# The first 1 MB of an expert's weights as two transfers of 64 partitions, one on each hardware queue

## The chip, the cores and the metric

The kernel runs on one core of a Trainium2 chip. The metric is the time of one execution on the device in microseconds (us); medians of several runs are quoted. A ratio is the mean time of one kernel's runs over the mean of the other's of the same rounds, so it is not quite the ratio of the medians that stand beside it.

## The reference

Windowed attention (8 batches, 8 heads, 576 positions, head size 64; four heads with a plain window, four with a dilated one) is followed by a soft mixture of experts with 8 experts of 4 slots each:

```python
attn_out = _attn_ref(q, k, v)                      # f32, [8, 8, 576, 64]
x = attn_out.transpose(0, 2, 1, 3).reshape(4608, 512)
logits = x @ phi                                   # phi [512, 32]
d = softmax(logits, axis=0); slot_input = (d.T @ x).reshape(8, 4, 512)
for e in range(8):                                 # w1 [8, 512, 1024], w2 [8, 1024, 512]
    slot_out[e] = np.maximum(slot_input[e] @ w1[e], 0.0) @ w2[e]
return softmax(logits, axis=1) @ slot_out.reshape(32, 512)
```

All inputs are f32 in HBM. The weights are 33.5 MB of them, q, k and v together 28.3 MB.

## The kernel before

GpSimd's software queue loads nearly everything and casts f32 to bf16 in flight. A small scheduler in Python orders the instructions of each engine; the order is fixed when the program is built. The first half of the columns of w1 of expert 0 is an exception: it is loaded as f32 on SyncE's hardware queue, which can start before GpSimd has issued anything (0.74 against 1.23 us), into a place that w2 of expert 0 fills much later. ScalarE casts it from there:

```python
def w1_rows(e):
    return moe_w1[e].rearrange("(p four) f -> p (four f)", four=4)   # 128 rows of 4096 f32
...
op(SP, lambda: spq.dma_start(
    af(w2off(0), [[1, 2048]]),            # f32 view, 128 partitions x 8 KB
    w1_rows(0)[:, :2048]), .1, -200.0,
   kind="dma", nbytes=1 << 20, sem=sem("s_w1f"), writes=b_w2[0], name="w1f")
for x in range(2):
    op(ACT, lambda x=x: act.activation(
        a(o_w1 + 1024 * x, [[1, 1024]]), af(w2off(0) + 2048 * x, [[1, 1024]]), ACTF.Copy),
        1.1, -200.0, reads=b_w2[0], writes=[b_w1[0]], name=f"w1c{x}")
...
wq += [w1_piece(e, 2 if e == 0 else 0) for e in range(8)]   # the rest of w1, on GpSimd
```

The softmax here doesn't subtract the row's maximum and nothing guards it: scores larger than these inputs give would overflow.

Of the kernel before, what the change touches and what calls it, by code (L numbers as in the profile page):

```python
# [58 lines left out]
class Sched:  # L59
# [8 lines left out]
    def op(self, eng, fn, dur, prio, reads=(), writes=(), rmw=(), after=(), banks=(), name="",  # L68
           kind="c", nbytes=0, rate=422e3, lag=0.0, sem=None, tail=False):
        o = Op()  # L70
        o.eng, o.fn, o.dur, o.prio, o.name = eng, fn, dur, prio, name
        o.kind, o.bytes, o.rate, o.lag, o.sem, o.tail = kind, nbytes, rate, lag, sem, tail
        o.deps, o.succ = set(), []
        o.banks, o.opens, o.ord = [], [], None
        o.seq = len(self.ops)
        for a in after:
            if a is not None:
                o.deps.add(a)
        for b in reads:
            o.deps.update(b.w)  # L80
            b.r.append(o)
        for b in writes:
            if b.r:
                b.prev = b.w + b.r
                b.w, b.r = [], []
            o.deps.update(b.prev)
            b.w.append(o)
        for b in rmw:
            o.deps.update(b.prev)
            o.deps.update(b.w)  # L90
            o.deps.update(b.r)
            b.w.append(o)
        for b in list(reads) + list(writes) + list(rmw) + list(banks):
            if isinstance(b, Bank) and b not in o.banks:
                o.banks.append(b)
                if b.left == 0:
                    o.opens.append(b)
                b.left += 1
        o.deps.discard(o)
        self.ops.append(o)  # L100
        return o
# [99 lines left out]
def bass_dilated_sliding_attn__then__soft_moe_slots_kernel(  # L201
# [66 lines left out]
    def af(off, dims, p0=0, pn=128):  # L268
        return AP(ar_f.tensor, (p0 * NBF + off) // 2, [[NBF // 2, pn]] + dims)
# [12 lines left out]
    op = sc.op  # L282
    PE, ACT, DVE, POOL, SP = "PE", "ACT", "DVE", "POOL", "SP"
    pe, act, dve, pool, spq = nc.tensor, nc.scalar, nc.vector, nc.gpsimd, nc.sync
# [26 lines left out]
    b_w2 = [[Buf(f"w2{e}{s}") for s in range(2)] for e in range(8)]  # L311
# [6 lines left out]
    def w2off(e):  # L318
        return o_w2 + e * 8 * DM if e < 5 else o_stg + (e - 5) * 8 * DM


    def sem(n):
        return [nc.alloc_semaphore(n), 0]
# [39 lines left out]
    def w1_rows(e):  # L363
        return moe_w1[e].rearrange("(p four) f -> p (four f)", four=4)
# [28 lines left out]
    def load_w(n):  # L393
# [11 lines left out]
                   writes=list(wr) + rd + ([x for y in b_kqv[0] for x in y] if name[:2] == "w2" and e in (3, 4) else []))  # L405


    op(SP, lambda: spq.dma_start(
        af(w2off(0), [[1, 2048]]),
        w1_rows(0)[:, :2048]), .1, -200.0,  # L410
       kind="dma", nbytes=1 << 20, sem=sem("s_w1f"), writes=b_w2[0], name="w1f")
    for x in range(2):
        op(ACT, lambda x=x: act.activation(
            a(o_w1 + 1024 * x, [[1, 1024]]), af(w2off(0) + 2048 * x, [[1, 1024]]), ACTF.Copy),
# [398 lines left out]
    for x, y in zip(dma_order, dma_order[1:]):  # L813
# [7 lines left out]
       writes=[b_rcol], name="cs")  # L821
# [17 lines left out]
    for x in range(2):  # L839
# [12 lines left out]
        for g in range(2):  # L852
# [5 lines left out]
            writes=[b_hsb[x], b_p[0], b_p[1]], name=f"RL{x}")  # L858
# [20 lines left out]
    def l2(es, x, col, n, cs=range(8), bufs=None):  # L879
# [22 lines left out]
       name="SOx")  # L902
# [153 lines left out]
```

## Time and profile before

| | before |
|---|---|
| median time | 177.12 us (176.88 to 177.25, 4 runs) |
| span of the profiled run | 175.2 us |
| DMA | 41.26 MB written by 14,388 packets, near 213 GB/s from 5 to 145 us |

The prediction below works with 177.03 us, the median of the first three of these runs. It shows the lines of the profile that carry the argument. One view more is needed later. It is the queue view of the first 12 us, whose columns are packets, MB, and the time that their packets took as a share of 16 engines over those 12 us:

```profile
q0 software_dynamic: 710, 1.47, 64.8%
q1 hardware_dynamic: 144, 1.05, 26.4%
```

The hardware queue's row is the transfer in question: 1.05 MB took 26.4% of 12 us, so 3.17 us of all 16 engines.

### The profile page before, as it was taken

To read this page: it belongs to the slowest core of one execution; us is meant where nothing else is said; L and a number is where in the kernel's file an instruction comes from. 1 tells how busy PE (TensorE), PEld (TensorE's weight loads), DVE (VectorE), ACT (ScalarE), POOL (GpSimd) and SP (SyncE) were. 2 spreads that over 40 slices of the span, in tenths; PEclk is the share of its full clock that TensorE was granted. 3 is DMA by queue.
4 is the path that set the end of the run, shared out by engine and by line. 5 is a ranking of instruction groups with operands and counts; after the bars stand their busy time and mean duration, and the time that the engine had idled before them with its cause. 6 is when DMAs were issued, how large, how long until landed. Compare 5 with 4: busy or idle time off the path is not lost.

```text
span 175.2 us, 4785 instructions
## 1 busy us (share of the span) xinstructions
PE 127.4 (73%) x2102; PEld 86.0 (49%) x2102; DVE 120.7 (69%) x220; ACT 105.1 (60%) x165; POOL 44.5 (25%) x90
## 2 busy tenths in 40 slices
PE   0008667969998998998988997999776766898000
PEld 0005535746766866776756766776343323442000
DVE  6899497978998998998698798349430002699300
ACT  2404763797978969969868968965603001599000
POOL 7659502406234053027200014940000000000000
PEclk9999995699999999999999999999999999999655
DMA  6999999999999999999999999999999999999997
GB/s 191 228 210 217 211 214 208 219 210 213 216 211 214 217 213 207 218 211 217 213 209 216 217 213 221 215 219 211 209 223 215 210 192 189 270 343 418 449 423 299
DMA packets 14388, 41.26 MB, mean 236 GB/s; under 512 B 1696, under 2 KB 7328, under 8 KB 12064
## 3 DMA queue, kind: packets, MB, share of 16 engines
q0 software_dynamic: 10512, 30.41, 88.3%
q1 hardware_dynamic: 3856, 10.55, 15.7%
q8 instruction: 16, 0.26, 0.5%
q14 instruction: 4, 0.03, 0.0%
HBM read 61.93 MB, written 9.44 MB: 407 GB/s over the span
## 4 chain that ended last, share of the span: by engine, by line
DMA 33%; DVE 24%; PE 22%; ACT 7%; POOL 5%; issue 3%; POOLq 0%; DVEq 0%
DMA ar<-in_moe_w_dram 21%; DMA ar<-in_v_dram 12%; PE ps L529 6%; DVE ar L497 6%; DVE ar L945 6%; ACT ar L568 4%; POOL ar L381 3%; DVE ar L503 3%; PE ps L590 2%; PE ps L713 2%; PE ps L536 2%; DVE ar L634 2%; PE ps L623 2%; PE ps L546 2%; DVE ar L454 2%
## 5 line engine op out<-in xcount | busy, mean ns | idle before, releaser
L568 ACT ACTIVATE ar<-ps 128x1152 bf16<-128x1152 f32 (+1 forms) x32 | 37.9, 1186 | 21.5 <-PE ps L553 10.9
L529 PE MATMUL ps<-ar 128*128 128x320 bf16 (+1 forms) x128 | 23.2, 306 | 16.1 <-DVE ar L503 13.8
L497 DVE STREAM_TRANSPOSE ar<-ar 128x576 uint32<-128x576 uint32 x28 | 32.8, 1237 | 0.6 <-DMA ar<-in_v_dram 0.6
L634 DVE TENSOR_TENSOR ar<-ps,fs 96x768 bf16<-96x768 f32 (+1 forms) x32 | 26.3, 822 | 1.1
L596 ACT ACTIVATE ar<-ps 128x768 bf16<-128x768 bf16 x32 | 24.8, 809 | 3.6 <-PE ps L590 3.1
L529 PEld LDWEIGHTS ps<-ar 128*128 128x128 bf16 x128 | 10.8, 100 | 20.9 <-POOL ar L427 13.7
L623 PE MATMUL ps<-ar 128*128 128x65 bf16 x320 | 15.2, 195 | 3.4 <-ACT ar L568 2.1
L590 PE MATMUL ps<-ar 128*128 128x128 bf16 x192 | 15.8, 229 | 2.4 <-DVE ar L634 2.1
L503 DVE STREAM_TRANSPOSE ar<-ar 128x576 uint32<-128x576 uint32 x12 | 14.6, 1241 | 1.8 <-DMA ar<-in_q_dram 1.8
L623 PEld LDWEIGHTS ps<-ar 128*128 128x128 bf16 x320 | 12.1, 98 | 6.7 <-ACT ar L568 2.9
L345 POOL DMA_DIRECT2D ar<-in_k_dram x14 | 7.5, 541 | 30.5 <-DVE ar L497 15.6
L942 ACT ACTIVATE ar<-ps,fs 128x512 f32<-128x512 f32 (+1 forms) x23 | 11.4, 636 | 5.7 <-PE ps L934 5.7
L590 PEld LDWEIGHTS ps<-ar 128*128 128x128 bf16 x192 | 12.7, 118 | 3.7 <-DVE ar L634 2.3
L630 DVE RECIPROCAL fs<-ps 96x12 f32<-96x12 f32 (+1 forms) x32 | 6.5, 203 | 10.9 <-PE ps L623 10.6
L885 PE MATMUL ps<-ar 128*32 128x512 bf16 (+1 forms) x76 | 10.8, 347 | 4.3 <-DMA ar<-in_moe_w_dram 3.3
L945 DVE TENSOR_SCALAR ar<-ps,fs 128x512 f32<-128x512 f32 (+1 forms) x23 | 12.7, 627 | 1.0 <-PE ps L934 1.0
L934 PE MATMUL ps<-ar 128*128 128x512 bf16 (+1 forms) x46 | 10.2, 346 | 1.1 <-DVE ar L909 1.0
L343 POOL DMA_DIRECT2D ar<-in_q_dram x16 | 8.8, 549 | 6.1 <-DVE ar L509 6.1
L713 PE MATMUL ps<-ar 128*128 128x288 bf16 x64 | 9.8, 299 | 0.7 <-ACT ar L697 0.7
L693 ACT ACTIVATE ar<-ps 128x1024 bf16<-128x1024 bf16 x8 | 8.2, 1030 | 3.3 <-PE ps L680 3.3
L690 ACT ACTIVATE ar<-ps 128x576 bf16<-128x576 bf16 x16 | 9.5, 648 | 1.1 <-PE ps L674 0.8
L509 DVE STREAM_TRANSPOSE ar<-ar 128x160 uint32<-128x160 uint32 (+1 forms) x32 | 9.6, 413 | 0.0
(78 smaller groups left out, 190.2 us busy)
## 6 DMA issues: line engine op xcount, KB each, us to landing
ar<-in_moe_w_dram POOLq DMA_DIRECT2D x13, 1024.0 KB, 26.6
ar<-in_k_dram POOLq DMA_DIRECT2D x16, 288.0 KB, 14.5
ar<-in_q_dram POOLq DMA_DIRECT2D x16, 288.0 KB, 16.2
ar<-in_v_dram POOLq DMA_DIRECT2D x16, 288.0 KB, 15.2
out_dram<-ar SPq DMA_DIRECT2D x2, 2048.0 KB, 10.1
out_dram<-ar SPq DMA_DIRECT2D x10, 256.0 KB, 3.1
out_dram<-ar SPq DMA_DIRECT2D x2, 1024.0 KB, 6.1
ar<-in_moe_w_dram SPq DMA_DIRECT2D x1, 1024.0 KB, 4.9
```

The lines of the kernel that those rows point to most:

```text
L497: return dve.transpose(au(o_kqv[kq] + 2304 * j + 36 * x, [[1, 18], [36, 16], [576, 2]]), au(src + 64 * 18 * x, [[32, 18], [1, 32]]))
L503: return dve.transpose(au(dst, [[1, 18], [18, 32]]), au(src, [[32, 18], [1, 32]]))
L529: pe.matmul(pf(h, 0, [[1, W]]), a(o_id, [[1, 128]]), a(msk, [[1, W]]), start=True, stop=False)
L568: eo = op(ACT, lambda P=P, W=W: act.activation(a(P, [[W, 4], [1, W]]), AP(ps, 0, [[4096, 128], [512, 4], [1, W]]), ACTF.Exp, scale=SCALE), ...
L590: last = pe.transpose(pb(bank.idx, bb * 256 + par * 32, [[64, 4], [1, 32]]), src, a(o_id, [[1, 128]]))
L596: op(ACT, lambda t=t, bank=bank: act.activation(a(o_vb[vs] + 3 * t * VBK, [[66, 12], [2, 32], [1, 2]]), pb(bank.idx, 0, [[64, 12], [1, 32] ...
L623: last = pe.matmul(pf(bank.idx + x, 65 * t, [[1, 65]]), w, a(VB + t * VBK + 66 * h, [[1, 65]]), start=True, stop=True)
L634: op(DVE, lambda hp=hp, bank=bank: dve.tensor_tensor(a(ox + 128 * hp, [[64, 2], [256, NT], [1, 64]], 0, rows), pf(bank.idx, 0, [[512, 2], ...
L713: last = pe.matmul(pf(bank.idx, 0, [[1, 288]]), a(o_phis + 128 * c, [[1, 128]]), a(o_xt[xt] + 576 * c + 288 * g, [[1, 288]]), start=(c == ...
L885: last = pe.matmul(pf(sobank[x].idx, 0, [[1, n]], 32 * j, 32), a(o_htz + 1024 * g + 128 * c + 32 * j, [[1, 32]]), a(w2off(e) + DM * c + co ...
L942: op(ACT, lambda: act.activation(dst, src(), ACTF.Copy, scale=sca), actt(cw, .1), prio + .1, reads=[bank, b_rinv], writes=wr, name=f"OE{G} ...
L945: op(DVE, lambda: dve.tensor_scalar(dst, src(), sca, None, op0=AluOp.mult), dvet(cw, True) + .08, prio + .1, reads=[bank, b_rinv], writes= ...
```

## The change

The intent is to feed the DMA engines from both hardware queues in the first microseconds. The 128 partitions are cut in two, 0 to 63 on SyncE's queue and 64 to 127 on ScalarE's:

```diff
-    op(SP, lambda: spq.dma_start(
-        af(w2off(0), [[1, 2048]]),
-        w1_rows(0)[:, :2048]), .1, -200.0,
-       kind="dma", nbytes=1 << 20, sem=sem("s_w1f"), writes=b_w2[0], name="w1f")
+    for e, dma, p0 in ((SP, spq, 0), (ACT, act, 64)):
+        op(e, lambda dma=dma, p0=p0: dma.dma_start(
+            af(w2off(0), [[1, 2048]], p0, 64), w1_rows(0)[p0:p0 + 64, :2048]), .1, -200.0 - (e == ACT),
+           kind="dma", nbytes=1 << 19, sem=sem(f"s_w1f{p0}"), writes=b_w2[0], name=f"w1f{p0}")
```

## The prediction

Passages of the recorded prediction that no trace or run of this case shows are cut, and the cuts are marked. Its sum came to 177.03 - 0.2 + 0 = 176.8 us. The sixteen small packets are in the trace of before: 4 bytes and 9 ns each, so 16 x 9 / 16 = 9 ns of all 16 engines, the 0.01 us that it takes as zero.

> **What bounds the kernel now.** I read four views in this order: the page (busy shares, slices, queues), the table of busy time by stage, the chain of waits that ended last, and the timelines of VectorE and ScalarE in the first 20 us. First the slices of the page:
>
> ```profile
> PE   0008667969998998998988997999776766898000
> DVE  6899497978998998998698798349430002699300
> DMA  6999999999999999999999999999999999999997
> GB/s 191 228 210 217 211 214 208 219 210 213 216 211 214 217 213 207 218 211 217 213 209 216 217 213 221 215 219 211 209 223 215 210 192 189 270 343 418 449 423 299
> ```
>
> One slice is 175.2 / 40 = 4.4 us. The reader is to see that only the DMA row is full from the second slice to the last but one; TensorE starts in the fourth slice and every compute engine has gaps. The rate is flat, near 213 GB/s, while f32 inputs are loaded as bf16, and rises past 400 when f32 output is stored. What was asked of the queue early also lands late:
>
> ```profile
> q0 software_dynamic: 10512, 30.41, 88.3%
> q1 hardware_dynamic: 3856, 10.55, 15.7%
> ar<-in_moe_w_dram POOLq DMA_DIRECT2D x13, 1024.0 KB, 26.6
> ```
>
> The queue lines are packets, MB and share of 16 engines; the third is KB per transfer and the median us from issue to landing. A 1 MB weight load lands 26.6 us after its issue, though at 213 GB/s it needs about 5: the rest is backlog. The chain of waits says the same at its end: 20.95 us on the v load that landed at 100.63, then
>
> ```profile
> 115.33 36.21 DMA ar<-in_moe_w_dram
> 151.54 0.04 issue
> ```
>
> and after that some 24 us of final products and stores. The POOL timeline has no load issued between 84.4 and 104.6, yet the stages 85 to 95 and 95 to 105 moved 214 and 219 GB/s; so the backlog is never empty. **The end is set by the start of the DMA stream plus its bytes over its rate.** The other half is the start. The chain from 0.73 to 13.63 is VectorE alone: memsets to about 10, then transposes, and TensorE begins at 13.76. No DMA stands on that part of the chain. ScalarE's timeline there is
>
> ```profile
> 0.74 1.28 ACT L413 ACT_TABLE_LOAD   x1 [0.74 <-PEq L1041]
> 5.67 2.00 ACT L413 ACTIVATE ar<-ar 128x1024 bf16<-128x1024 f32 x2 [3.65 <-DMA ar<-in_moe_w_dram]
> 15.53 1.13 ACT L568 ACTIVATE ar<-ps 128x1152 bf16<-128x1152 f32 x1 [7.86 <-PE ps L536]
> ```
>
> It waits 3.65 us for the transfer that the change splits, casts it in 2.00 us to 7.67, and then is idle for 7.86 us until the first scores. What the split can give or take at this spot has 7.86 us of slack behind it. Last, the table in half-microseconds, from which the only possible gain is read (columns after the clock: DMA share of 16 engines, GB/s):
>
> ```profile
> 1.00:1.50 0.50, 0.00 (x0) 0.00 (x0) 0.22 (x2) 0.50 (x1) 0.27 (x1) 1.00 0.00 0
> 1.50:2.00 0.50, 0.00 (x0) 0.00 (x0) 0.50 (x1) 0.50 (x1) 0.50 (x2) 1.00 1.23 213
> 2.00:2.50 0.50, 0.00 (x0) 0.00 (x0) 0.50 (x1) 0.02 (x1) 0.50 (x2) 1.00 0.52 115
> 2.50:3.00 0.50, 0.00 (x0) 0.00 (x0) 0.35 (x1) 0.00 (x0) 0.50 (x2) 1.00 0.93 246
> 3.00:3.50 0.50, 0.00 (x0) 0.00 (x0) 0.37 (x1) 0.00 (x0) 0.50 (x2) 1.00 0.77 328
> 3.50:4.00 0.50, 0.00 (x0) 0.00 (x0) 0.50 (x1) 0.00 (x0) 0.50 (x2) 1.00 0.87 360
> 4.00:4.50 0.50, 0.00 (x0) 0.00 (x0) 0.50 (x2) 0.00 (x0) 0.50 (x3) 1.00 1.09 459
> ```
>
> The DMA engines start at 1.5 us, and between 2.0 and 4.0 they are not quite full, while this one transfer and the first k, q and v loads are in flight.
>
> [...]
>
> **The change part by part.**
>
> *Removed:* one issue of 1 MB on SyncE, 0.37 us long, landing 4.9 us after its start at 0.74, so at about 5.6.
>
> *Added:* two issues of 64 partitions and 0.5 MB, one on SyncE and one on ScalarE. Bytes are the same 1.05 MB, rows the same 8 KB. The queue view of the first 15 us counts 144 packets on the hardware queue, 128 rows and, as I read it, 16 completions; two transfers would make 160. Sixteen packets that carry almost nothing[...], cost in the order of 0.01 us of the stream, which I take as zero.
>
> *On ScalarE:* the issue, 0.37 us[...], at a time when it sits idle anyway.
>
> *Moved:* the compiled streams of the two kernels show the same instructions in the same order on TensorE, VectorE and GpSimd. On ScalarE the cast now needs two semaphores, and the compiler puts the wait for the first half on the table load and that for the second half on the cast. So the table load, which ran under the transfer from 0.74 to 2.02, now follows the first half's landing. If both halves still land by 5.6, the casts start at 5.6 + 1.28 = 6.9 and end at 8.9, 1.2 us later than now. If the halves land 1 us sooner, they end at 7.9. Either is at least 6.6 us ahead of 15.53, where ScalarE is next needed. **Cost on the path: 0.** The second half of this expert's weights goes straight to other columns and depends on neither; the scratch place that the casts free is refilled only by a w2 load issued after 82 us.
>
> *The early k, q, v loads:* issued from 1.23 on, with 5.8 to 8.3 us (k), 6.5 to 9.2 (q), 7.4 to 10.1 (v) to landing, so the first k is there at about 7.0 and the last v at about 14.1. VectorE takes them at 10.57 and 16.66. The smallest slack is some 2.5 us. If the hardware queues go first, the loads lose at most the weights' remaining time at full rate, under 1 us. Hidden.
>
> *The gain:* how much idle DMA time in 1.5 to 4.0 the second ring can fill. Steady shares are about 1.08 in this view; the five half-microseconds sum to (1.23 + 0.52 + 0.93 + 0.77 + 0.87) x 0.5 = 2.16 of 2.5 x 1.08 = 2.70. At most **0.54 us** is to be had, and since the backlog never empties, what is had there comes through to the end. I expect a third of it, since part is the first read's latency and the software queue's slow start[...]: about 0.2 us.
>
> Sum: 177.03 - 0.2 + 0 = **176.8 us**.
>
> **The rivals.**
>
> *A: the transfer was waiting on one ring, and two fill the hole fully.* For it: ScalarE's 3.65 us wait and the 0.52 share at 2.0 to 2.5. Against it: at 4.0 to 4.5 the engines are full anyway, and the loads behind were already queued. It would give 177.03 - 0.54 = 176.5. Much more would need a path that waits for this weight, and the chain has none.
>
> *B: the table load moved behind the wait becomes a delay.* For it: 1.28 us more on ScalarE in series. Against: the 7.86 us of idle time after. Even if ScalarE lost the whole 1.28 on the path, 178.3, still under 1%; I give it very little.
>
> *C: the second queue has a cost outside the instructions:* set-up[...], or uneven engines with 64 partitions. The timed median of 177.03 is 1.8 us above the span, and an extra queue could add some tenths there. Nothing in the trace speaks for it, and nothing excludes it. It would make 177.2 to 177.6.
>
> *D: the reordered start shifts the later load issues,* since GpSimd issues as buffers come free. For it: long idle times before its issues (5.6, 7.9 and 20.2 us at longest). Against: the backlog of tens of microseconds absorbs such shifts. Some tenths either way.
>
> **Range and chances.** The three runs of before lie within 176.88 and 177.20. I allow A's full gain plus half a microsecond of D below, and C with D above: 176.1 to 177.7. 2% is 3.5 us; the early hole holds 0.54 and the largest serial cost found is 1.28, so neither side reaches it: faster 0.02, within 2% 0.96, slower 0.02.
>
> **What would show it right or wrong.** In the profile after: two issues near 0.74 on SyncE and ScalarE; the table load after 4 us and the casts ending before 9; a DMA share nearer 1.08 from 2.0 to 4.0, with the hardware queue's bytes in earlier; VectorE's first transposes still at about 10.6 and TensorE at about 13.8; a flat 213 GB/s to the last weights at about 151.3. It would be wrong if the chain began with the weights or with ScalarE's casts, if a load made VectorE wait before 14 us, if the rate of the middle stages moved by over 1%, or if the span stayed while the timed median moved, which would be C.

## The result, and the profile after

The changed kernel takes **178.91 us** (178.80 to 179.04, 4 runs) against 177.12 us: 1.79 us slower, a ratio of 1.0101 with a 95% interval of 1.0086 to 1.0117. The class "within 2%" was right; the time lies outside the range of 176.1 to 177.7.

First the slices of the page of the changed kernel, the same rows as before:

```profile
DMA  6999999999999999999999999999999999999996
GB/s 139 200 209 214 211 209 216 220 207 212 220 209 210 218 214 208 215 216 207 217 217 208 214 220 220 211 213 224 213 213 218 214 189 192 264 334 414 448 429 296
```

The DMA row is as full as before, but the first two slices moved 139 and 200 GB/s where they had moved 191 and 228. A slice is 4.4 us, so this is (52 + 28) GB/s x 4.4 us = 0.35 MB that is still to be loaded at 9 us; at 213 GB/s that is 1.7 us. Nothing of such a size differs afterwards. The half-microsecond table of the changed kernel (last two columns: DMA share of 16 engines, GB/s) shows where in those slices:

```profile
1.50:2.00 0.50, 0.00 (x0) 0.00 (x0) 0.50 (x1) 0.00 (x0) 0.50 (x2) 1.00 0.00 0
2.00:2.50 0.50, 0.00 (x0) 0.00 (x0) 0.50 (x1) 0.00 (x0) 0.50 (x2) 1.00 1.48 262
2.50:3.00 0.50, 0.00 (x0) 0.00 (x0) 0.35 (x1) 0.00 (x0) 0.50 (x2) 1.00 0.81 246
3.00:3.50 0.50, 0.00 (x0) 0.00 (x0) 0.36 (x1) 0.00 (x0) 0.50 (x2) 1.00 0.81 213
3.50:4.00 0.50, 0.00 (x0) 0.00 (x0) 0.50 (x1) 0.00 (x0) 0.50 (x2) 1.00 1.14 262
4.00:4.50 0.50, 0.00 (x0) 0.00 (x0) 0.50 (x2) 0.00 (x0) 0.50 (x3) 1.00 1.20 262
```

From 4.0 to 4.5 the engines are busy, share 1.20, and move 262 GB/s; before, they moved 459 at a share of 1.09. **A busy DMA engine is not a moving one:** the same bytes occupy it longer. Also nothing starts before 2.0, where before a start at 1.5 to 2.0 was seen. The queue view of the first 12 us puts a number on it:

```profile
q0 software_dynamic: 533, 1.11, 49.1%
q10 hardware_dynamic: 80, 0.52, 20.2%
q1 hardware_dynamic: 80, 0.52, 19.0%
```

The two halves took 20.2% + 19.0% = 39.2% of 12 us, 4.70 us of all engines, for the bytes that took 3.17 us before. That is 1.53 us more. The trace also keeps every packet's start, duration, queue and size. In these records a packet of 8 KB on the hardware queue took 309 ns in the middle before, and 597 ns after.

ScalarE's timeline shows the moved table load, and that it costs nothing:

```profile
6.04 1.28 ACT L413 ACT_TABLE_LOAD   x1 [6.04 <-DMA ar<-in_moe_w_dram]
8.58 2.00 ACT L413 ACTIVATE ar<-ar 128x1024 bf16<-128x1024 f32 x2 [1.26 <-DMA ar<-in_moe_w_dram]
15.53 1.13 ACT L568 ACTIVATE ar<-ps 128x1152 bf16<-128x1152 f32 x1 [4.95 <-PE ps L536]
```

The second half lands at 8.58, the casts end 2.9 us later than before, and the first scores come at 15.53 as before, with 4.95 us of idle time ahead of them. VectorE and TensorE also start as before, to 0.01 us up to 20 us. At the far end, the chain of waits has the row of final evictions, before and then after:

```profile
152.84 8.63 DVE ar L945 x15
```

```profile
154.60 8.64 DVE ar L945 x15
```

They begin 1.76 us later and take as long. So compute was not delayed at the start, and the whole loss stands at the end. What lies between is the stream. Set against each other packet by packet, the software queue's packet of the same number starts later in the changed kernel by

```text
packet at (us, before):   4.8   8.3  13.2  29.6  58.6  87.3  129.7  148.1
later after the change:  1.53  1.73  1.78  1.69  1.74  1.72   1.83   1.77
```

(Packets of 4 bytes are left out of the count.) The lag is 1.53 us with the first packet and 1.73 by 8.3 us, and is neither absorbed nor much increased in the next 140 us.

### The profile page after: what moved, and what is told of

It reads as the page before. It is cut to its first block, busy times and chain, and to the rows that moved or that the text cites. A ratio compares the mean times of both kernels' runs of the same rounds, so it can differ in the third digit from the quotient of the medians.

```text
span 177.0 us, 4787 instructions
## 1 busy us (share of the span) xinstructions
PE 127.7 (72%) x2102; PEld 85.8 (48%) x2102; DVE 121.3 (69%) x220; ACT 105.2 (59%) x165; POOL 44.6 (25%) x90
## 4 chain that ended last, share of the span: by engine, by line
DMA 45%; DVE 25%; PE 11%; ACT 4%; POOL 4%; issue 3%; POOLq 0%; DVEq 0%
DMA ar<-in_v_dram 24%; DMA ar<-in_moe_w_dram 21%; DVE ar L497 8%; DVE ar L945 6%; PE ps L529 3%; ACT ar L568 3%; DVE ar L503 3%; POOL ar L381 2%; DVE ar L454 2%; DVE ar L634 2%; PE ps L590 1%; ACT ar L596 1%; PE ps L536 1%; POOL ar L345 1%; DVE ar L459 1%
## 5 line engine op out<-in xcount | busy, mean ns | idle before, releaser
L529 PEld LDWEIGHTS ps<-ar 128*128 128x128 bf16 x128 | 10.8, 101 | 20.3 <-POOL ar L427 13.7
```

Of the source, the lines that this page charges most:

```text
L529: pe.matmul(pf(h, 0, [[1, W]]), a(o_id, [[1, 128]]), a(msk, [[1, W]]), start=True, stop=False)
```

## The experiments

The theory, called P in the expectations, is that it matters where a transfer writes: one whose partitions all lie within 0 to 63, or all within 64 to 127, takes up to twice as long for each f32 packet of 8 KB, and one with partitions of both sets does not. The packet records say where to look. A transfer of 64 partitions still keeps 16 packets under way at once, as the whole one does: 16 or 17 of the first half's at any time from 2.4 to 4.0 us, 16 or 17 of the whole one's from 2.75 to 4.75. Each half ends with 16 packets of 4 bytes, as the whole transfer does. Those of the second half come 2.26 to 2.43 us after those of the first, taken in order, which is what four rows of 597 ns one after another take (2.39). So as many packets run at once and each of them is slow; no record names an engine. The halves did go one after the other: the first starts its packets from 2.05 to 4.43 us, the second from 4.01 on, and the loads behind from 6.29. The runs test P by its packet times and total times alone.

The rivals were: a second hardware queue slows the stream (Q); ScalarE's queue is slow by itself (A); any 64-partition transfer is slow (N); the table load behind the wait is the cost (T); the reads or the shape, not the writes, are the cost (R).

The packet records of each kernel are gathered here, so that each section below can be short. "us of engines" is the hardware queues' share of the first 12 us (in e7, both transfers), times 12; "lag" is the median delay of the software queue's packets against the kernel before; "time" is the difference from the median of before in the same rounds.

```text
kernel             first packet  median 8 KB packet  us of engines   lag    time
before                 1.74 us        309 ns             3.17        0       0
changed                2.05           597                4.70       1.77   +1.79
e1_both_on_sync        2.06           606                4.91       2.01   +1.92
e2_columns             1.75           159 (4 KB)         3.18       0.02   -0.02
e3_whole_on_act        1.75           309                3.19       0.08   +0.13
e4_middle              1.76           374                3.54       0.34   +0.88
e5_even_odd            2.08           309                3.34       0.45   +0.54
e6_one_semaphore       2.08           606                4.61       1.75   +1.92
e7_twice               1.75           322                5.71       2.58   +2.61
e8_cast_halves         1.76           309                3.10       0.02   +0.34
```

### Both halves on SyncE

```diff
-    for e, dma, p0 in ((SP, spq, 0), (ACT, act, 64)):
+    for e, dma, p0 in ((SP, spq, 0), (SP, spq, 64)):
```

> Both halves (partitions 0-63, 64-127) issued from SyncE, one after the other: one hardware queue, same shape as the changed kernel. Theory P ([...]each 8 KB packet takes nearly twice as long): still slow, 8 KB packets mostly 550-640 ns against 309 before, first software-queue packet after 6.0 us, median 178.4 to 178.9. Theory Q (a second hardware queue slows the stream): packets 309 ns again, 177.0 to 177.3. Part of the loss[...] (first packet 0.3 us later): gone here, so about 0.3 us less than the changed kernel under P.

Measured: 179.04 us (178.85 to 179.18), ratio 1.0109 (1.0096 to 1.0122), with one hardware queue. Its queue view of the first 12 us:

```profile
q0 software_dynamic: 510, 1.06, 47.5%
q1 hardware_dynamic: 160, 1.05, 40.9%
```

1.05 MB on one queue took 40.9%, as slow as on two. So the second queue isn't the cause. One part of the expectation missed: I had put the later start down to SyncE and ScalarE issuing at the same time. Here SyncE issues both, and the first packet still starts at 2.06. The two issues took 1.18 us together; that of before took 0.37. The later start goes with transfers of 64 rows. So the time, 179.04, lies above the expected 178.4 to 178.9, and nothing of the 0.3 us was won back. A second part missed as well: the first software-queue packet started at 3.92 and not after 6.0, since here the loads behind ran in between the second half's packets. The sum was the same.

### Two queues, split by columns

```diff
+    for e, dma, c0 in ((SP, spq, 0), (ACT, act, 1024)):
+        op(e, lambda dma=dma, c0=c0: dma.dma_start(
+            af(w2off(0) + 2 * c0, [[1, 1024]]), w1_rows(0)[:, c0:c0 + 1024]), .1, -200.0 - (e == ACT), ...
```

> Two transfers, one on each hardware queue, as in the changed kernel, but split by columns: each has all 128 partitions and rows of 4 KB. Theory P: fast, packets of 4 KB near 155-165 ns, 177.1 to 177.6 (the later start of about 0.3 us may stay). Theory Q: slow as the changed kernel, 178.6 to 179.0.

Measured: 177.10 us (177.00 to 177.37), ratio 1.0001 (0.9989 to 1.0014).

```profile
q1 hardware_dynamic: 144, 0.52, 13.8%
q10 hardware_dynamic: 144, 0.52, 12.7%
```

Two queues and two transfers, the table load behind its wait as in the changed kernel, but 128 partitions in each: 26.5% for the same bytes, as before. Theory Q falls. So does the gain I had hoped for: the table in half-microseconds has a share of 0.61 at 2.0 to 2.5 in this run as well, so a second ring did not fill the hole of the start.

### The whole transfer on ScalarE

```diff
-    op(SP, lambda: spq.dma_start(
+    w1f = op(SP, lambda: act.dma_start(
...
     order = sc.run([4, 5, 6, 7], [0, 1, 2, 3], last_ex[0])
+    w1f.eng = ACT
+    order.remove(w1f)
+    order.insert(0, w1f)
```

(The lines below the scheduler's run keep every other instruction in its place.)

> The transfer of before, whole, but issued from ScalarE alone. Everything else in the same order. Both theories: as before, 176.9 to 177.3, since one queue and 128 partitions. If ScalarE's queue is slow by itself (theory A), 178 or more, with packets over 309 ns. Issue near 0.37 us if the 0.54 and 0.57 of the changed kernel were contention.

Measured: 177.25 us (176.92 to 177.34), ratio 1.0003 (0.9991 to 1.0015), an issue of 0.38 us. ScalarE's queue is as good as SyncE's; theory A falls.

### Partitions 32 to 95, then the two outer quarters

```diff
+    for e, dma, p0, n in ((SP, spq, 32, 64), (ACT, act, 0, 32), (SP, spq, 96, 32)):
+        op(e, lambda dma=dma, p0=p0, n=n: dma.dma_start(
+            af(w2off(0), [[1, 2048]], p0, n), w1_rows(0)[p0:p0 + n, :2048]), .1, -200.0 - (e == ACT), ...
```

> Three transfers: partitions 32-95 (64) first from SyncE, then 0-31 from ScalarE and 96-127 from SyncE (32 each). Theory P[...]: 32-95[...] 64 packets take 309 ns; the two of 32[...] 500-640 ns. Half of the changed kernel's packet loss: 177.7 to 178.3. Rival N (a 64-partition transfer is slow because of its number of partitions, wherever they lie): 32-95 as slow as the halves, 550-640 ns, and 178.7 or more in time. Theory Q: as slow as the changed kernel too, all packets alike.

Measured: 178.00 us, in two groups of three runs (177.53 to 177.67 and 178.32 to 178.48), ratio 1.0050 (1.0033 to 1.0068). ScalarE's issue was the shorter (0.39 against 0.58 us), so its quarter went first, from 1.76 us. The 64 packets of partitions 32 to 95 settle, in their second half, at 309 to 345 ns; the first half fell into the slow start that every kernel here has (118 to 182 GB/s, the mean of the first three slices of 0.3 us in which anything moved, against 410 to 437 in four later slices of the kernel before). The last 32, of partitions 96 to 127, begin at 322 ns and then go at 360 to 549, but for two. So 64 partitions that lie on both sides of 64 are not slow. The quarter 0 to 31 fell into that start and says little: even in the kernel before, the packets that start before 2.0 us take 756 ns on average. Yet 12 of its 32 packets took 330 ns or less, where 500 to 640 had been expected. The lag of 0.34 us is nearer to the faster group of runs, 0.50 us above before. In the profiled run, of the slower group, the lag was still 0.31 at 148.6 us, but the final evictions began 1.26 us later than before (154.10 against 152.84): some 0.9 us more was lost where loads give way to stores. What caused that was not found.

### Even partitions on one queue, odd on the other

```diff
-    for e, dma, p0 in ((SP, spq, 0), (ACT, act, 64)):
+    for e, dma, p0 in ((SP, spq, 0), (ACT, act, 1)):
-            af(w2off(0), [[1, 2048]], p0, 64), w1_rows(0)[p0:p0 + 64, :2048]), ...
+            AP(ar_f.tensor, (p0 * NBF + w2off(0)) // 2, [[NBF, 64], [1, 2048]]), w1_rows(0)[p0:128:2, :2048]), ...
```

> As the changed kernel, two transfers of 64 partitions with rows of 8 KB on the two hardware queues, but the even partitions on one and the odd on the other. Theory P: [...]packets lie between: 309 to 500 ns, and the time well below the changed kernel, 177.1 to 178.0. Rival N (64 partitions in one transfer are slow wherever they lie): packets 560-640 ns, 178.6 to 179.0.

Measured: 177.56 us (177.43 to 177.75), ratio 1.0031 (1.0017 to 1.0045).

```profile
q1 hardware_dynamic: 80, 0.52, 17.3%
q10 hardware_dynamic: 80, 0.52, 10.5%
```

This differs from the changed kernel in nothing but which partitions go together. The second queue's half, which runs after the slow start, took 10.5% where it took 20.2%. Theory N falls. I had expected packets of up to 500 ns; past 3.5 us they took 309 to 322 ns, but for a few. What stays, 0.54 us, adds up: packets 3.34 - 3.17 = 0.17 us, and a start at 2.08 in place of 1.74, 0.34 us. The two issues took 0.54 and 0.56 us, so the later start again goes with transfers of 64 rows, wherever they lie.

### One semaphore for both halves

```diff
+    s_w1f = sem("s_w1f")
     for e, dma, p0 in ((SP, spq, 0), (ACT, act, 64)):
...
-sem=sem(f"s_w1f{p0}")
+sem=s_w1f
```

> The changed kernel with both halves counting on one semaphore, so that the cast needs one wait and ScalarE's table load is not behind it: the load is back at about 0.8-1.4 us, the casts start about when the second half lands (8.6). Theory P (the loss is in the DMA stream): 178.7 to 179.1, as the changed kernel. Theory T (the table load moved behind the wait costs its 1.28 us on the path): 177.4 to 177.8.

Measured: 178.94 us (178.82 to 178.97), ratio 1.0106 (1.0093 to 1.0120). ScalarE's timeline:

```profile
1.35 1.28 ACT L414 ACT_TABLE_LOAD   x1 [1.35 <-PEq L1042]
8.41 2.00 ACT L414 ACTIVATE ar<-ar 128x1024 bf16<-128x1024 f32 x2 [5.78 <-DMA ar<-in_moe_w_dram]
```

The table load is back under the transfer, and the time has not moved. Theory T falls, and the prediction's cost of 0 for it is shown.

### One more megabyte at the start

```diff
+    twice = op(SP, lambda: spq.dma_start(
+        af(w2off(1), [[1, 2048]]), w1_rows(1)[:, :2048]), .1, -199.0,
+       kind="dma", nbytes=1 << 20, sem=sem("s_twice"), name="twice")
+    for x in b_w2[1]:
+        x.prev = [twice]
```

(The last two lines make the load that fills this place later wait for the added one.)

> The kernel before with one more 1 MB transfer of the same shape (128 partitions, 8 KB rows) right behind the first on SyncE, into a place that is filled again later; the result stays correct. It adds 128 packets of 309 ns on 16 engines = 2.47 us to the start of the stream and nothing to any compute engine. If what the stream loses early arrives whole at the end (theory P needs that for its 1.8 us): the software queue's packets lag 2.4-2.5 us throughout and the time is 179.4 to 179.7. If early delay is absorbed by slack further on: under 178.5, and theory P would not explain the changed kernel's time.

Measured: 179.63 us (179.55 to 179.78), ratio 1.0148 (1.0134 to 1.0161).

```profile
q1 hardware_dynamic: 288, 2.10, 47.6%
```

The added transfer raised this share from 26.4% to 47.6%, which is 2.54 us of engines more; the software queue lagged by 2.58 us and the end came 2.61 us later. Early stream time arrives whole, with every compute instruction as before. This is why 1.5 us of slower packets and a 0.3 us later start are 1.8 us at the end.

### Halves in the software queue, which writes bf16

```diff
-W_AFTER = [1, 0, 1, 1, 1, 1, 1, 99]
+W_AFTER = [1, 0, 2, 2, 2, 1, 1, 99]
...
+    def w1_half(e, p0):
+        def fn():
+            return pool.dma_start(a(o_w1 + e * 4096, [[1, 4096]], p0, 64), w1_rows(e)[p0:p0 + 64])
+        return (fn, 2 << 19, f"w1_{e}p{p0}", [b_w1[e]])
...
-    wq += [w1_piece(e, 2 if e == 0 else 0) for e in range(8)]
+    wq += [x for e in range(8) for x in ([w1_half(e, 0), w1_half(e, 64)] if e in (1, 2, 3) else [...])]
```

(W_AFTER counts the weight loads that are issued after each batch's inputs; two halves count as two, so each weight keeps its place.)

> The kernel before with the loads of w1 of experts 1, 2 and 3 (2 MB read, 1 MB written as bf16, each) split into partitions 0-63 and 64-127 in the same software queue. In the kernel before these 8 KB writes take 625 ns a packet, so each engine writes 13.1 bytes per ns, half of the 26.5 of the f32 transfer. Theory P: [...]packets stay near 625-660 ns and the time 176.9 to 177.6. Rival R (a half-range transfer is slow for its reads or for its shape, whatever it writes): packets near 1,200 ns, and three loads of 5 us each double to about +15 us.

Measured: 177.36 us (177.06 to 177.54), ratio 1.0017 (1.0003 to 1.0030). The packets of these three loads took 625 ns in the middle, 624 to 625 from the 5th to the 95th percentile, exactly as unsplit. Each reads 16 KB and writes 8 KB. This speaks against theory R: six halves of the same 64 partitions, with twice the bytes read, cost the stream nothing (lag 0.02). So do e4 and e5, whose transfers on the hardware queue also read 64 rows of 8 KB and settled near 309 ns. What differs from the changed kernel is the rate of writing. The software queue's packets write 8192 / 625 = 13.1 bytes per ns, halves or not. The f32 packets of the hardware queue write 8192 / 309 = 26.5 when whole, and 8192 / 597 = 13.7 in the halves. An estimate from these three: if a packet of a half can write no more than about 13.7 bytes per ns, e8's 13.1 stay within it and the f32 packets do not. The run changes the queue along with the rate, so it doesn't exclude that the software queue deals with halves in another way. The 0.3 us of time without a lag is not explained; the interval only just leaves out no difference. In the profiled run the final evictions begin 0.26 us later than before (153.10), but in that of e2, whose median equals before, they do so by 0.29 without a lag too.

## Why the prediction was wrong

- **What bounds the kernel** was right, and it is what turned a small fault into time: the end follows the DMA stream's start and its rate. The lag of 1.7 to 1.8 us over 140 us shows it, and e7 shows it by intervention.
- **The step that failed is "Added".** It said "Bytes are the same 1.05 MB, rows the same 8 KB" and counted only 16 packets more. It assumed that the same bytes and rows cost the same engine time. They did not: 4.70 us in place of 3.17. The view that I used, packets and bytes by queue, can't see which partitions a packet writes, and I did not ask that for a change that is all about partitions. One of the prediction's signs of being right even came true for the wrong reason: the DMA share from 2.0 to 4.0 rose from 0.77 to 1.06 on average, near the 1.08 that was asked for, while the rate fell from 262 to 246 GB/s.
- **The later start** was missed too. I counted ScalarE's issue as 0.37 us of idle time and let nothing of it reach the stream. An issue of 64 rows itself takes 0.54 to 0.58 us against 0.37 to 0.42 for 128 rows, and the first packet comes 0.31 us later. It was no wait of one engine's issue for the other's: in e1 one engine alone took 0.54 and 0.58, and in e2 both issued at 0.74 us and took 0.38 and 0.40 us. The number of rows alone doesn't set it either: e4's two issues of 32 rows took 0.39 us on ScalarE and 0.56 on SyncE. Together 1.53 + 0.31 = 1.84, where the lag is 1.77 and the time 1.79.
- **The gain** of "about 0.2 us" is not there. With the fault taken away (e2), two queues give -0.02 us: the hole at 2.0 to 4.0 stays with two rings. The prediction had misread the hole: it has the k, q and v loads in flight there, but in the kernel before their first packet starts at 4.77 us. Until then the split transfer has the DMA engines to itself. What it called the first read's latency and the software queue's slow start is there before the change (issued at 0.74, first packet at 1.74, and 756 ns on average for the 13 packets that start before 2.0; the first software load issued at 1.23, first packet at 4.77), and the split of e2 left the first of these as it was (first packet at 1.75).
- **Rival C** named "uneven engines with 64 partitions" but gave it some tenths in all, outside the instructions. It came nearest, mis-sized: the loss goes with these transfers of 64 partitions, but is 1.8 us and inside the stream. That the engines are uneven is not shown. Rivals A, B and D had no part; e2, e6 and the constant lag show that.
- **The loads behind.** The prediction let them lose the weights' remaining time if the hardware queues go first. In the changed kernel each half went as a block: the second half's first row starts at 4.01 us, as the first half's first packet of 4 bytes comes (4.00), and the software queue's first at 6.29, as the second half's first of 4 bytes does. The k, q and v loads took 2.1 us longer to land (k from 5.8-8.3 to 7.9-10.4). The estimate of "under 1 us" was short, but the slack of 2.5 us just held: the last v landed at about 16.3, the prediction has VectorE take it at 16.66, and VectorE and TensorE started as before.
- **ScalarE** was right in kind: the casts ended at 10.58 in place of the expected 8.9, with cost 0.

What is shown: the loss is in the stream, and it goes with which partitions share a transfer; it isn't the queue, the semaphore or the number of partitions. What makes a packet slow when its transfer keeps to one side of partition 64 is not shown: no record names an engine or a place in the memory. That it goes by side fits the settled packets of all ten kernels and, with the estimate above, the free halves of e8. During the slow start some packets ran at 309 ns in the halves too (12 of the changed kernel's first 64 took 330 or less). Why 64 rows take longer to issue, and why the two halves were served one after the other, stays open. No experiment pointed to a version that beats the kernel before; the best of them equal it.

## What to carry to other kernels

If a full-rate transfer has to be split, try columns before partition ranges: here two halves by columns cost nothing (-0.02 us) and two ranges of 64 partitions 1.79 us on two queues and 1.92 on one. When the DMA stream is the bound and never runs dry, count its engine time by packet duration and not by bytes or busy share: here 2.54 us of engine time added at the start (e7) came out as 2.61 us at the end. And look for the lag between matching packets of two traces: its size, and where it first appears, say where to look for the cause.
